# First batch's attention: exponentials turned by TensorE in float32 in place of float16 halves turned by DMA

## The chip, the cores and the metric

The kernel runs on one core of one Trainium2 chip. Five engines work beside each other, each through its own queue in order: TensorE (PE, its weight loads shown apart as PEld), VectorE (DVE), ScalarE (ACT), GpSimd (POOL) and SyncE (SP), which issues the DMAs here. They wait for each other by semaphores. The metric is the device time of one execution in microseconds (us); less is better.

## The reference

Clustered attention over 2 batches x 8 heads x 768 positions x 64 dimensions, then two feed-forward layers over the 1536 tokens.

```python
q_assign = np.argmax(np.einsum('bhsd,hcd->bhsc', q_n, c_n), axis=-1)   # q_n, k_n, c_n: normalised
k_assign = np.argmax(np.einsum('bhsd,hcd->bhsc', k_n, c_n), axis=-1)
mask = q_assign[:, :, :, None] == k_assign[:, :, None, :]
scores = np.where(mask, scale * np.matmul(q, k.transpose(0, 1, 3, 2)), -1000000000.0)
attn = np.exp(scores - np.max(scores, axis=-1, keepdims=True))
attn = attn / (np.sum(attn, axis=-1, keepdims=True) + 1e-09)
x = np.matmul(attn, v)                    # then tokens x 512
h = x @ w_in                              # 512 -> 2048
x = (h * np.clip(h + 3.0, 0.0, 6.0) / 6.0) @ w_out
for e in range(4):                        # 4 experts, 512 -> 1024 -> 512
    out += p[:, e:e + 1] * (np.maximum(x @ w1[e], 0.0) @ w2[e])
```

`w_in` and `w_out` arrive as 64-bit floats and are turned into 32-bit ones on the chip.

## The kernel before

The program is written as a list of tasks, each for one engine with an assumed duration, a due time (`prio`) and the buffers that it reads and writes. `Order.plan` places them one by one, by these assumed durations, and `emit` writes the instructions in that order. So the order of each queue is fixed beforehand, and a change of one task or of one assumed duration moves others. The table `PAR` holds due times, pool sizes and choices of engine.

The stages are: attention of the first batch (`a0`), the first layer of the first batch (`Moe1`, with the conversion of `w_in` and `w_out`, `conv_w`), its second layer (`Moe2`) with the attention of the second batch (`a1`) in its gaps, and the two layers of the second batch. Attention goes by pairs of heads (4) and blocks of 256 queries (3 a pair): 12 blocks, each of 4 units (2 heads x 128 queries), 48 units in all.

One unit of the first batch runs so:

- `scores` (L708): PE writes 128 x 768 scores into a tile `pss` (two PSUM banks, ring `ps_sa` of three) by four matmuls (L718, L720). Ahead of them stands a matmul of zeros, 384 columns wide, that is overwritten (`fill`, L716). DVE takes the row maximum (L725), ACT the exponential with the row sum (L726) into the float32 tile `e`.
- `sums` (L731): two one-column DVE instructions give the reciprocal of the row sum (L734, L735).
- `halves` (L737): the normalised `e` is written as two float16 tiles, the rounded value and the rest. By its letter in `ka` a unit does so as "P" (POOL L740, ACT L741, POOL L742), as "A" (ACT L745, DVE L749) or as "D" (POOL L747, DVE L749).
- a DMA transpose (L681, on SP's queue) turns the halves into `pt`.

When a block's four units are turned, `av` (L694) multiplies with `v`: 18 steps of two matmuls (one for each head, side by side in 64 columns of the array), since high and low halves of `pt` and of `v` make three products over six blocks of keys. L702 (ACT) and L704 (DVE) write the block's result `x1` as a rounded and a rest part. `values` (L628) loads `v` and makes its halves `vh` and `vl` (L636 to L655). `prep` (L516) makes ready what the scores of a pair read.

`conv_w` (L786) converts a tile of `w_in` or `w_out`: DMA load (L791), ACT L794, DVE L795, L796, L798, L800. Four of the 32 tiles fall in the attention stage, the other 28 behind it.

Of the kernel before, what the change touches and what calls it, by code (L numbers as in the profile page):

```python
# [25 lines left out]
def _f32(u):  # L26
# [23 lines left out]
    lead1=2.4290359447307104,  # L50
    vlead=-11.709535254235975,
    avp=-9.142989452549473,
    parts=3,
    ka=["APDPPDPDADPA", "PADPPAPAAPAP", "PPDPPDDAAPAA", "PDPDPDPDPPAD"],
    kb="DDDP",
    a_pool=dict(raw=2, nat=3, vr=1, sc=1, so=1, cs=2, oh=3, sm=2, e=6, p=3, pt=4, vh=2, vl=2, tiny=11, tv=4, stk=4),
    b_pool=dict(raw=2, nat=1, vr=1, sc=2, so=1, cs=1, oh=1, sm=2, e=2, p=2, pt=3, vh=1, vl=1, tiny=11, tv=4, stk=2),
    xba=[2, 2, 2, 1, 2, 1, 1, 2, 1, 2, 2, 1],
    xbb=1,
    loa="VP",  # L60
    lob="VV",
# [4 lines left out]
    nat0=-49.95,  # L66
    dup=["PPPP", "P"],
    dpx=2,
    fill=384,
    wo1=0,  # L70
    two=[0, 0],
    seq=[0, 1, 3, 2, 4, 5, 6, 7, 9, 10, 8, 11],
    btail=10.347963191960837,
    bu0=39.36802588487378,
# [258 lines left out]
def body(ctx: ExitStack, tc: tile.TileContext, qk, nat, vd, cent, w_in, w_out, probs, w1, w2, out):  # L333
# [23 lines left out]
    def pe(n, prio, fn, r, w, cols=0):  # L357
        return add("PE", n, prio, fn, r, w, cols=cols or 2400 * n)
# [4 lines left out]
    def dve(n, prio, fn, r, w, fast=False, ap=False):  # L363
        return add("DVE", 1e-3 * (n / (1.92 if fast else 0.96) + 68 + 60 * ap), prio, fn, r, w)

    def pool(n, prio, fn, r, w, ns=2.1):
        return add("POOL", 1e-3 * (n * ns + 150), prio, fn, r, w)

    def dma(nbytes, prio, fn, r, w):
        return add("SP", 0.52, prio, fn, r, w, dma=nbytes / 360e3)  # L370

    mm = lambda n: 1e-3 * (n / 2.4 + 2.5)


    g_c = o.group("left", keep=True)
# [22 lines left out]
    p_x2 = {n: Pool(f"x2{n}", 1, g_w) for n in "hl"}  # L398
    p_oa = Pool("oa", 1, g_w)
    p_g = Pool("g", 5, g_w1)  # L400
    p_s = [Pool("ps_sa", 3, g_pa, True), Pool("ps_sb", 2, g_ps, True)]
    p_v = [Pool("ps_va", 1, g_pa, True), Pool("ps_vb", 1, g_ps, True)]
    p_pm = [Pool("ps_ma", 1, g_pa, True), Pool("ps_mb", 3, g_pm, True)]
    p_m = p_pm[1]
# [71 lines left out]
    x1 = {}  # L476

    class Attn:
        def __init__(self, b, g, gp, n):
            self.b = b  # L480
            self.xb = max(PAR["xba"]) if b == 0 else PAR["xbb"]
            prep = ("raw", "nat", "vr", "sc", "so", "cs", "oh", "sm")
            P = lambda name: Pool(name + str(b), n[name], gp if name in prep else g)
            self.p = {k: P(k) for k in ("raw", "nat", "vr", "sc", "so", "cs", "oh", "sm", "e", "p", "pt", "vh", "vl", "tiny", "tv")}
            if b == 0:
                self.p["ohq"] = Pool("ohq", 1, gp)
            for k in ("qa", "qb", "ka", "kb"):
# [140 lines left out]
        def values(self, hp, p):  # L628
            b, st = self.b, self.pair[hp]
            vr = self.buf("vr", [128, 2, NT, D], F32)  # L630
            dma(393e3, p(0), lambda: nc.sync.dma_start(out=vr.t, in_=vd[b, hp]), [], [vr])
            tb = self.buf("tv", [128, 8], F32)
            am, inv, mx, dg = tb, tb, tb, tb
            vh, vl = self.buf("vh", [128, 2, NT, D], F16), self.buf("vl", [128, 2, NT, D], F16)
            for q in range(2):
                act(HS, p(1), lambda q=q: nc.scalar.activation(out=vh[:, q], in_=vr[:, q], func=AF.Abs, accum_out=am[:, q:q + 1]),  # L636
                    [vr], [(vh, q), (tb, 0)], acc=True)
            ps = Buf(p_pm[b], [2, 128], F32, "psam")
            pe(0.1, p(1), lambda: nc.tensor.transpose(ps.t, am[:, 0:2], ident.t), [(tb, 0)], [ps])
# [12 lines left out]
            for q in range(2):
                act(HS, p(2), lambda q=q: nc.scalar.activation(out=vh[:, q], in_=vr[:, q], func=AF.Copy, scale=inv[:, 6 + q:7 + q]),
                    [vr, (tb, 3)], [(vh, q)], ap=True)
                dve(HS, p(2), lambda q=q: nc.vector.scalar_tensor_tensor(  # L655
                    out=vl[:, q], in0=vr[:, q], scalar=inv[:, 6 + q:7 + q], in1=vh[:, q], op0=ALU.mult, op1=ALU.subtract),
                    [vr, (tb, 3), (vh, q)], [(vl, q)], ap=True)
            st["v"] = (vh, vl)

        def block(self, hp, blk, p, kinds, xb, avp):  # L660

# [69 lines left out]
        def sums(self, tb, n, p):  # L731
            keys = [(tb, 2 + i) for i in range(n)]
            rs = lambda: tb[:, 2:2 + n]
            dve(n, p, lambda: nc.vector.tensor_scalar(out=rs(), in0=rs(), scalar1=1e-9, scalar2=1.0 / PSC, op0=ALU.add, op1=ALU.mult), [], keys)  # L734
# [296 lines left out]
    for hp in range(NP):  # L1031
        t0 = when[hp, 0]
        lead = lambda x, t0=t0, hp=hp: t0 - (G["lead0"] + G["lead2"] * hp - G["lead1"] * x) if hp else -49.9 + 0.1 * x
        a0.prep(hp, lead, G["loa"] if hp else "VV")
        a0.values(hp, (lambda x, t0=t0: t0 - G["vlead"] - G["vlead2"] * hp + x) if hp else (lambda x: 3.0 + x))
        for blk in range(NBQ):
            a0.block(hp, blk, lambda i, t0=when[hp, blk]: t0 + i * T_UNIT, G["ka"][hp][4 * blk:4 * blk + 4], G["xba"][3 * hp + blk], G["avp"])

    t = T_A + NP * per * T_UNIT + 4.0
    stages = []  # L1040
# [125 lines left out]
```

## Time and profile before

| | |
|---|---|
| device time, median of 3 runs | 1071.14 us (1069.41 to 1074.32) |
| span of the profiled execution, first to last instruction | 1070.8 us |
| PE busy | 981.9 us (92%) |
| DVE busy | 781.6 us (73%) |
| ACT busy | 517.5 us (48%) |
| POOL busy | 496.9 us (46%) |
| mean granted TensorE clock | 0.962 of full speed |

The profile gives no time of the profiled execution but its span, which stands 0.3 us under the median of the runs. Busy shares are means over stages that differ, so stages are read apart. A granted clock of 1.0 is 2.4 GHz, 0.5 is 1.2 GHz; a value between is a mean over a stretch that had both. Busy times of PE are those of overlapping matmuls, so PE's rate is read from the starts of matmuls that follow each other.

### The profile page before, as it was taken

To read this page: it belongs to the slowest core of one execution; us is meant where nothing else is said; L and a number is where in the kernel's file an instruction comes from. 1 tells how busy PE (TensorE), PEld (TensorE's weight loads), DVE (VectorE), ACT (ScalarE), POOL (GpSimd) and SP (SyncE) were. 2 spreads that over 40 slices of the span, in tenths; PEclk is the share of its full clock that TensorE was granted. 3 is DMA by queue.
4 is the path that set the end of the run, shared out by engine and by line. 5 is a ranking of instruction groups with operands and counts; after the bars stand their busy time and mean duration, and the time that the engine had idled before them with its cause. 6 is when DMAs were issued, how large, how long until landed. Compare 5 with 4: busy or idle time off the path is not lost.

```text
span 1070.8 us, 15706 instructions
## 1 busy us (share of the span) xinstructions
PE 981.9 (92%) x5579; PEld 881.4 (82%) x5579; DVE 781.6 (73%) x1407; ACT 517.5 (48%) x969; POOL 496.9 (46%) x385
## 2 busy tenths in 40 slices
PE   3666787889899999999999999999999999999998
PEld 1555666788799888888898898999999999899987
DVE  8999995999635687478467356679888577766773
ACT  6676765545336446345255343565554334443330
POOL 3576963555346787255263444533442313333221
PEclk9777789899999999999999999999999999999999
DMA  8499799866205476257357347512221112212211
GB/s 262 108 194 193 152 180 219 265 206 221 69 1 169 148 164 150 90 142 142 99 132 129 97 97 167 138 42 77 62 86 50 62 58 79 80 48 71 76 44 59
DMA packets 192366, 129.34 MB, mean 121 GB/s; under 512 B 155488, under 2 KB 155488, under 8 KB 192288
## 3 DMA queue, kind: packets, MB, share of 16 engines
q1 hardware_dynamic: 192288, 128.34, 46.5%
q8 instruction: 44, 0.72, 0.3%
q14 instruction: 34, 0.28, 0.1%
HBM read 74.51 MB, written 11.53 MB: 80 GB/s over the span
## 4 chain that ended last, share of the span: by engine, by line
PE 51%; DVE 24%; DMA 10%; issue 6%; POOL 5%; ACT 3%; SPq 0%; POOLq 0%; DVEq 0%; ACTq 0%
PE psm L814 8%; PE psm L816 8%; PE psm L815 8%; DMA pt<-p 7%; DVE p L749 4%; PE psw L886 4%; PE psw L884 4%; PE psw L885 4%; PE psg L815 4%; PE psg L816 3%; PE psg L814 3%; DVE ut L725 3%; DVE wconv L795 2%; DVE wconv L798 2%; DVE wconv L800 2%
## 5 line engine op out<-in xcount | busy, mean ns | idle before, releaser
L758 POOL TENSOR_TENSOR w<-wraw,w 128x512 fp32r<-128x512 f32 x160 | 215.3, 1372 | 276.8 <-ACT w L757 269.9
L814 PE MATMUL psm<-w,h 128*128 128x512 f32 x384 | 152.0, 396 | 0.8 <-DVE h L997 0.8
L816 PE MATMUL psm<-w,h 128*128 128x512 f32 x384 | 150.8, 393 | 0.0
L815 PE MATMUL psm<-w,h 128*128 128x512 f32 x384 | 150.5, 392 | 0.0
L726 ACT ACTIVATE e<-pss,ut 128x768 f32<-128x768 f32 x96 | 86.0, 897 | 72.4 <-DVE ut L725 50.7
L757 ACT ACTIVATE w<-wraw 128x512 fp32r<-128x512 f32 x160 | 95.1, 627 | 25.7 <-DMA wraw<-in_w 12.2
L1012 DVE SCALAR_TENSOR_TENSOR oa<-psm,pr,oa 128x512 f32<-128x512 f32 x84 | 61.7, 746 | 56.2 <-PE psm L816 56.1
L749 DVE SCALAR_TENSOR_TENSOR p<-e,ut,p 128x768 f16<-128x768 f32 x62 | 87.5, 1417 | 19.0 <-POOL p L747 16.0
L814 PE MATMUL psm<-x2h,w 128*128 128x384 f32 x288 | 98.3, 341 | 0.6 <-DVE h L997 0.6
L816 PE MATMUL psm<-x2h,w 128*128 128x384 f32 x288 | 96.8, 336 | 0.0
L815 PE MATMUL psm<-x2l,w 128*128 128x384 f32 x288 | 96.5, 335 | 0.0
L815 PE MATMUL psg<-g,w 128*128 128x384 f32 x256 | 88.5, 346 | 6.0 <-DVE g L951 4.4
L725 DVE TENSOR_REDUCE ut<-pss 128x1 f32<-128x768 f32 x96 | 90.1, 945 | 4.6 <-PE pss L720 4.5
L814 PE MATMUL psg<-g,w 128*128 128x384 f32 x256 | 87.8, 343 | 3.2 <-DVE t L946 2.3
L816 PE MATMUL psg<-g,w 128*128 128x384 f32 x256 | 87.2, 341 | 1.7 <-POOL w L758 1.7
L814 PEld LDWEIGHTS psm<-w,h 128*128 128x128 f32 x384 | 72.1, 188 | 16.8 <-issue 1.8
L816 PEld LDWEIGHTS psm<-w,h 128*128 128x128 f32 x384 | 72.1, 188 | 16.0 <-DVE h L997 0.2
L815 PEld LDWEIGHTS psm<-w,h 128*128 128x128 f32 x384 | 72.2, 188 | 12.8
L997 DVE SCALAR_TENSOR_TENSOR h<-psm,h 128x384 fp32r<-128x384 f32 x72 | 39.6, 553 | 46.6 <-ACT h L996 46.5
L996 ACT ACTIVATE h<-psm 128x384 fp32r<-128x384 f32 x72 | 34.8, 487 | 79.3 <-PE psm L816 76.6
L747 POOL TENSOR_SCALAR p<-e,ut 128x768 f16<-128x768 f32 x49 | 47.0, 961 | 54.8 <-DMA pt<-p 24.4
L718 PEld LDWEIGHTS pss<-ka,qa 128*128 128x128 f32 x192 | 40.6, 220 | 30.8 <-issue 27.6
(185 smaller groups left out, 2508.2 us busy)
## 6 DMA issues: line engine op xcount, KB each, us to landing
wraw<-in_w SPq DMA_DIRECT2D x128, 256.0 KB, 3.2
r<-in_w_in SPq DMA_DIRECT2D x16, 512.0 KB, 4.9
r<-in_w_out SPq DMA_DIRECT2D x16, 512.0 KB, 4.4
nat<-in_nat SPq DMA_DIRECT2D x16, 384.0 KB, 4.1
raw<-in_qk SPq DMA_DIRECT2D x16, 384.0 KB, 4.0
scr_i<-wconv SPq DMA_DIRECT2D x16, 256.0 KB, 2.3
scr_o<-wconv SPq DMA_DIRECT2D x16, 256.0 KB, 3.0
wraw<-scr_i SPq DMA_DIRECT2D x16, 256.0 KB, 2.8
```

Of the source, the lines that this page charges most:

```text
L725: dve(S, p, lambda: nc.vector.tensor_reduce(out=nb(), in_=ps[:, :, 0:HS], axis=AX.XY, op=ALU.max, negate=True), [ps], [(tb, n)])
L726: act(S, p, lambda: nc.scalar.activation(out=e.t.rearrange("p (a b) -> p a b", a=2), in_=ps[:, :, 0:HS], func=AF.Exp, bias=nb(), scale=1.0 ...
L747: pool(S, p, lambda: nc.gpsimd.tensor_scalar(out=pp[:, j, 0], in0=e.t, scalar1=rs(), scalar2=1.0, op0=ALU.mult, op1=ALU.mult), [e, key], [ ...
L749: dve(S, p, lambda: nc.vector.scalar_tensor_tensor(out=pp[:, j, 1], in0=e.t, scalar=rs(), in1=pp[:, j, 0], op0=ALU.mult, op1=ALU.subtract) ...
L757: act(512, p, lambda: nc.scalar.activation(out=w[:, 0], in_=raw.t, func=AF.Copy), [raw], [(w, 0)])
L758: pool(512, p, lambda: nc.gpsimd.tensor_tensor(out=w[:, 1], in0=raw.t, in1=w[:, 0].bitcast(F32), op=ALU.subtract), [raw, (w, 0)], [(w, 1)])
L814: nc.tensor.matmul(o_, ah, bh, start=i == 0, stop=False)
L815: nc.tensor.matmul(o_, ah, bl, start=False, stop=False)
L816: nc.tensor.matmul(o_, al, bh, start=False, stop=i == 3)
L884: nc.tensor.matmul(o_, ah, bh, start=k == 0, stop=False)
L885: nc.tensor.matmul(o_, ah, bl, start=False, stop=False)
L1012: dve(512, p, lambda: nc.vector.scalar_tensor_tensor(out=oa[:, t], in0=ps.t, scalar=q, in1=oa[:, t], op0=ALU.mult, op1=ALU.add), [ps, pr], ...
```

## The change

For the first batch `block` gives way to `turned`. POOL normalises `e` in place in float32 for all 48 units. PE turns it by six float32 transposes a unit (L693 of the changed kernel) into two PSUM tiles `pst` of 384 columns (a ring of two); ACT (L700) and, for every fifth, DVE (L702) copies them to a float32 `pt`. `av` (L709) is then six steps of two float32 matmuls with `v` as it was loaded. The halves of `e` and of `v`, the scaling of `v` and the DMA transposes are gone for this batch. The matmul of zeros is gone (`fill=0`). The ring of scores goes from three tiles to two, which makes room for `pst`. The planner's assumed duration of every matmul rises by 10.5 ns (`mm`), so orders shift elsewhere too. The second batch's attention keeps its halves.

```diff
+    avpa=-8.0,
-    ka=["APDPPDPDADPA", "PADPPAPAAPAP", "PPDPPDDAAPAA", "PDPDPDPDPPAD"],
+    kn="PPPPPP",
+    kt="AAAAD",
-    a_pool=dict(raw=2, nat=3, vr=1, sc=1, so=1, cs=2, oh=3, sm=2, e=6, p=3, pt=4, vh=2, vl=2, tiny=11, tv=4, stk=4),
+    a_pool=dict(raw=2, nat=3, vr=3, sc=1, so=1, cs=2, oh=3, sm=2, e=7, pt=5, tiny=11, stk=4),
-    xba=[2, 2, 2, 1, 2, 1, 1, 2, 1, 2, 2, 1],
-    fill=384,
+    fill=0,
+    trp=3.0,
+    trh=2,
+    parta=6,
...
-    mm = lambda n: 1e-3 * (n / 2.4 + 2.5)
+    mm = lambda n: 1e-3 * (n / 2.4 + 13.0)
...
-    p_s = [Pool("ps_sa", 3, g_pa, True), Pool("ps_sb", 2, g_ps, True)]
+    p_s = [Pool("ps_sa", 2, g_pa, True), Pool("ps_sb", 2, g_ps, True)]
+    p_tr = Pool("ps_ta", PAR["trh"], g_pa, True)
...
             dma(393e3, p(0), lambda: nc.sync.dma_start(out=vr.t, in_=vd[b, hp]), [], [vr])
+            if b == 0:
+                st["v"] = vr
+                return
...
+        def turned(self, hp, blk, p, avp):
+            b, st = self.b, self.pair[hp]
+            pts, vr = [], st["v"]
+            for q in range(2):
+                qa, qb, ka, kb = st["heads"][q]
+                ptile = self.buf("pt", [128, JQ, NT, 128], F32)
+                pts.append(ptile)
+                for j in range(JQ):
+                    i = q * JQ + j
+                    tb = self.buf("tiny", [128, 8], F32, "ut")
+                    e = self.scores(qa, qb, ka, kb, blk * BQ + j * 128, tb, 0, p(i))
+                    self.sums(tb, 1, p(i), 1.0)
+                    sc = lambda eng, e=e, tb=tb: eng.tensor_scalar(out=e.t, in0=e.t, scalar1=tb[:, 2:3], scalar2=1.0, op0=ALU.mult, op1=ALU.mult)
+                    if PAR["kn"][i % len(PAR["kn"])] == "P":
+                        pool(S, p(i), lambda sc=sc: sc(nc.gpsimd), [(tb, 2)], [e], ns=0.956)
...
+                    nh = PAR["trh"]
+                    for h in range(nh):
+                        ps = Buf(p_tr, [128, 2 // nh, 512], F32, "pst")
+                        def turn(e=e, ps=ps, h=h):
+                            for t in range(NT // nh):
+                                x = (h * (NT // nh) + t) * 128
+                                nc.tensor.transpose(ps[:, t // 3, t % 3 * 128:t % 3 * 128 + 128], e[:, x:x + 128], ident.t)
+                        pe(NT // nh * 0.109, p(i) + PAR["trp"], turn, [e], [ps], NT // nh * 128)
...
+                        if PAR["kt"][((blk * 4 + i) * nh + h) % len(PAR["kt"])] == "A":
+                            act(S // nh, p(i) + PAR["trp"], lambda src=src, dst=dst: nc.scalar.activation(out=dst(), in_=src(), func=AF.Copy), [ps], [key], ps=True)
+                        else:
+                            dve(S // nh, p(i) + PAR["trp"], lambda src=src, dst=dst: nc.vector.tensor_copy(out=dst(), in_=src()), [ps], [key])
+            ps = Buf(p_v[b], [128, BQ], F32, "psv")
+            parts = PAR["parta"]
+            def av(part):
+                for t in range(part * NT // parts, (part + 1) * NT // parts):
+                    for q in range(2):
+                        nc.tensor.matmul(ps[64 * q:64 * q + 64], vr[:, q, t], pts[q][:, :, t], start=t == 0, stop=t == NT - 1)
...
-            a0.block(hp, blk, lambda i, t0=when[hp, blk]: t0 + i * T_UNIT, G["ka"][hp][4 * blk:4 * blk + 4], G["xba"][3 * hp + blk], G["avp"])
+            a0.turned(hp, blk, lambda i, t0=when[hp, blk]: t0 + i * T_UNIT, G["avpa"])
```

Three places show how the queues change. First PE in the later part of the stage. Before, each unit is a weight load and matmul of zeros (`junk`) and the four score matmuls, and between units stands a block's run of 36 float16 matmuls, of which the first pair of rows is shown:

```order
L716 LDWEIGHTS ident_b
L716 MATMUL pss<-junk,ident_b 128x384
L718 MATMUL pss<-ka,qa 128x384 x2
L720 MATMUL pss<-kb,qb 128x384 x2
L694 LDWEIGHTS vh
L694 MATMUL psv<-pt,vh 64x256
```

Now six transposes of an older unit stand between the scores of two units, and a block's product with `v` is one row of twelve matmuls:

```order
L693 MATMUL pst<-ident,e 128x128 x6
L778 MATMUL pss<-ka,qa 128x384 x2
L780 MATMUL pss<-kb,qb 128x384 x2
L709 MATMUL psv<-pt,vr 64x256 x12
L693 MATMUL pst<-ident,e 128x128 x6
```

PE has no row of zeros left, and gets one row of transposes for each unit. Second, SP at the end of the stage, where the loads of the first `w_out` tiles (`r`) stand. Before:

```order
L681 DMA_TRANSPOSE pt<-p 128x12x128
L681 DMA_TRANSPOSE pt<-p 128x24x128 x6
L681 DMA_TRANSPOSE pt<-p 128x12x128 x8
L791 DMA r_2032<-in_w_out 128x1024
L791 DMA r_2034<-in_w_out 128x1024
```

Now they follow the last small copies (`so` to `qb`, `kb`) of the fourth pair's preparation:

```order
L630 DMA qb<-so 16x768
L630 DMA kb<-so 16x768
L851 DMA r_1927<-in_w_out 128x1024
L851 DMA r_1929<-in_w_out 128x1024
```

The loads had the last 15 DMA transposes ahead of them, and have none now. Third, DVE from the stage's last row maximum (`ut<-pss`) to the first row of the 28 conversions (`wconv`). Before:

```order
L725 TENSOR_REDUCE ut<-pss 128x1
L749 SCALAR_TENSOR_TENSOR p<-e,ut,p 128x768
L735 RECIPROCAL ut<-ut 128x1
L734 TENSOR_SCALAR ut<-ut 128x1
L735 RECIPROCAL ut<-ut 128x1
L704 SCALAR_TENSOR_TENSOR x1l_710<-psv,sv,x1h_698 128x256
L734 TENSOR_SCALAR ut<-ut 128x1
L735 RECIPROCAL ut<-ut 128x1
L749 SCALAR_TENSOR_TENSOR p<-e,ut,p 128x768
L946 SCALAR_TENSOR_TENSOR t<-t,psg_1846 128x384
L749 SCALAR_TENSOR_TENSOR p<-e,ut,p 128x768
```

Two further `x1l` and `t` rows follow there before `wconv`. Now, with `t<-t,psg` the first layer's rows as before:

```order
L785 TENSOR_REDUCE ut<-pss 128x1
L794 TENSOR_SCALAR ut<-ut 128x1
L795 RECIPROCAL ut<-ut 128x1
L794 TENSOR_SCALAR ut<-ut 128x1
L795 RECIPROCAL ut<-ut 128x1
L717 TENSOR_TENSOR x1l_616<-psv,x1h_606 128x256
L702 COPY pt<-pst 128x384
L1006 SCALAR_TENSOR_TENSOR t<-t,psg_1748 128x384
L1006 SCALAR_TENSOR_TENSOR t<-t,psg_1853 128x384
L855 TENSOR_SCALAR wconv<-wconv 128x512
L856 TENSOR_SCALAR wconv<-wconv 128x512
L717 TENSOR_TENSOR x1l_616<-psv,x1h_606 128x256
```

The three rows L749 are gone from between, and the conversions now stand ahead of the last block's `x1l`.

## Rows read from the trace of the kernel before

**Rows 1.** Stretches: length, busy PE PEld DVE ACT POOL, granted clock, DMA share, GB/s.

```profile
26.40:161.40 135.00, 97.77 (x617) 76.84 (x618) 129.62 (x246) 94.32 (x174) 94.58 (x68) 0.76 0.82 165
161.40:183.90 22.50, 17.01 (x152) 14.16 (x151) 9.75 (x20) 11.63 (x21) 8.95 (x8) 0.92 0.93 191
183.90:282.00 98.10, 84.92 (x437) 78.38 (x436) 96.42 (x145) 48.83 (x91) 48.27 (x33) 0.95 0.67 219
290.00:1071.00 781.00, 765.92 (x4288) 700.08 (x4286) 521.11 (x937) 343.38 (x655) 333.50 (x264) 1.00 0.36 95
```

**Rows 2.** Timeline of DVE, first conversion instruction behind the attention stage.

```profile
183.38 0.43 DVE L795 TENSOR_SCALAR wconv<-wconv 128x512 f32<-128x512 f32 x1 [1.71 <-ACT wconv L794]
```

**Rows 3.** Timeline of PE, the first and the last unit's scores: start, length.

```profile
26.38 1.09 PE L718 MATMUL pss<-ka,qa 128*128 128x384 f32 x2
...
160.86 0.65 PE L718 MATMUL pss<-ka,qa 128*128 128x384 f32 x2
```

**Rows 4.** Groups by line, 26.4 to 161.4 us: busy, mean ns, idle before.

```profile
L742 POOL TENSOR_TENSOR p<-e,p 128x768 f16<-128x768 f32 x20 | 35.9, 1800 | 5.7 <-ACT p L741 5.4
L749 DVE SCALAR_TENSOR_TENSOR p<-e,ut,p 128x768 f16<-128x768 f32 x22 | 35.6, 1631 | 0.4 <-POOL p L747 0.4
L740 POOL TENSOR_SCALAR e<-e,ut 128x768 f32<-128x768 f32 x20 | 22.7, 1136 | 19.6 <-DVE ut L735 6.9 <-ACT e L726 5.9 <-DVE ut L734 3.8
L716 PE MATMUL pss<-junk,ident_b 128*128 128x384 bf16 x48 | 19.6, 408 | 26.7 <-ACT e L726 26.6
L741 ACT ACTIVATE p<-e 128x768 f16<-128x768 f32 x20 | 16.7, 840 | 9.0 <-POOL e L740 6.7 <-DMA pt<-p 2.2
L747 POOL TENSOR_SCALAR p<-e,ut 128x768 f16<-128x768 f32 x12 | 12.6, 1047 | 3.3 <-DMA pt<-p 2.0 <-issue 1.1 <-POOL e L740 0.2
L745 ACT ACTIVATE p<-e,ut 128x768 f16<-128x768 f32 x11 | 10.3, 932 | 3.5 <-DMA pt<-p 2.0 <-DVE ut L735 1.1 <-ACT e L726 0.2
L655 DVE SCALAR_TENSOR_TENSOR vl<-vr,tv,vh 128x384 f16<-128x384 f32 x8 | 8.3, 1072 | 0.8 <-ACT vh L653 0.8
L653 ACT ACTIVATE vh<-vr,tv 128x384 f16<-128x384 f32 x8 | 4.5, 605 | 4.0 <-DVE tv L651 4.0
L565 ACT ACTIVATE sc<-psc 128x384 f32<-128x384 f32 x3 | 1.5, 488 | 2.3 <-PE psc L562 2.3
```

**Rows 5.** The chain that ended last, 140 to 190 us.

```profile
167.82 5.45 DMA pt<-p
...
178.56 6.01 DMA r<-in_w_out
```

**Rows 6.** Timeline of SP's queue at the end of the attention stage.

```profile
151.49 25.94 SPq L681 DMA_TRANSPOSE pt<-p  x10
177.48 2.48 SPq L791 DMA_DIRECT2D r<-in_w_out  x4
```

**Rows 7.** The tile `pss`: who works on it, durations ns min/median/max.

```profile
L725 DVE TENSOR_REDUCE ut<-pss x96: 930/946/959, 28.9 to 668.6; 128x1 f32<-128x768 f32 x96
L726 ACT ACTIVATE e<-pss,ut x96: 877/901/910, 30.5 to 669.7; 128x768 f32<-128x768 f32 x96
L726 ACT ACTIVATION_READ_ACCUMULATOR e<-pss,ut x96: 184/192/211, 31.3 to 670.5; 128x1 f32 x96
```

**Rows 8.** Timeline of PE at clock 1.0, later: scores, float32 matmuls, transposes.

```profile
603.89 0.85 PE L562 MATMUL psc<-raw,ct 128*32 128x384 f32 x8
...
612.36 0.49 PE L570 MATMUL psct<-ident,sc 128*128 128x128 f32 x3
...
625.81 0.52 PE L718 MATMUL pss<-ka,qa 128*128 128x384 f32 x2
...
626.51 0.40 PE L814 MATMUL psm<-w,h 128*128 128x512 f32 x1
```

**Rows 9.** One tile's instructions: durations ns min/median/max (`psct`, then `psc`).

```profile
L570 PE MATMUL psct<-ident,sc x24: 270/272/476, 11.5 to 612.6; 128*128 128x128 f32 x24
...
L562 PE MATMUL psc<-raw,ct x64: 486/510/849, 7.4 to 604.3; 128*32 128x384 f32 x64
```

More of the change, by code (lines that the diff above doesn't have):

```diff
@@ L480, in __init__ @@
             self.b = b
-            self.xb = max(PAR["xba"]) if b == 0 else PAR["xbb"]
-            prep = ("raw", "nat", "vr", "sc", "so", "cs", "oh", "sm")
+            self.xb = PAR["xbb"]
+            prep = ("raw", "nat", "sc", "so", "cs", "oh", "sm") + (("vr",) if b else ())
             P = lambda name: Pool(name + str(b), n[name], gp if name in prep else g)
-            self.p = {k: P(k) for k in ("raw", "nat", "vr", "sc", "so", "cs", "oh", "sm", "e", "p", "pt", "vh", "vl", "tiny", "tv")}
+            self.p = {k: P(k) for k in n if k != "stk"}
             if b == 0:
@@ L658, in values @@
             st["v"] = (vh, vl)
+        def turned(self, hp, blk, p, avp):
[14 more added lines that the diff above has]
+                    else:
+                        dve(S, p(i), lambda sc=sc: sc(nc.vector), [(tb, 2)], [e], fast=True)
+                    nh = PAR["trh"]
[6 more added lines that the diff above has]
+                        pe(NT // nh * 0.109, p(i) + PAR["trp"], turn, [e], [ps], NT // nh * 128)
+                        src = lambda ps=ps: ps[:, :, 0:HS]
+                        dst = lambda ptile=ptile, j=j, h=h: ptile[:, j].rearrange("p (a t) k -> p a (t k)", a=2)[:, h * 2 // nh:(h + 1) * 2 // nh] if nh == 1 else ptile[:, j].rearrange("p (a t) k -> p a (t k)", a=2)[:, h:h + 1]
+                        key = (ptile, (j, h))
+                        if PAR["kt"][((blk * 4 + i) * nh + h) % len(PAR["kt"])] == "A":
+                            act(S // nh, p(i) + PAR["trp"], lambda src=src, dst=dst: nc.scalar.activation(out=dst(), in_=src(), func=AF.Copy), [ps], [key], ps=True)
+                        else:
+                            dve(S // nh, p(i) + PAR["trp"], lambda src=src, dst=dst: nc.vector.tensor_copy(out=dst(), in_=src()), [ps], [key])
[5 more added lines that the diff above has]
+                        nc.tensor.matmul(ps[64 * q:64 * q + 64], vr[:, q, t], pts[q][:, :, t], start=t == 0, stop=t == NT - 1)
+            for part in range(parts):
+                pe(NT / parts * (BQ * 4 / 2400 + 0.02), p(4 + part * 4 / parts) + avp, lambda part=part: av(part), pts + [vr], [ps], NT / parts * BQ * 4)
+            sl = slice(blk * BQ, blk * BQ + BQ)
+            xh, xl = x1[b]
+            key = (hp, blk)
+            act(BQ, p(6), lambda: nc.scalar.activation(out=xh[:, hp, sl], in_=ps.t, func=AF.Copy), [ps], [(xh, key)], ps=True)
+            dve(BQ, p(6), lambda: nc.vector.tensor_tensor(
+                out=xl[:, hp, sl], in0=ps.t, in1=xh[:, hp, sl].bitcast(F32), op=ALU.subtract), [ps, (xh, key)], [(xl, key)])
@@ L729, in scores, with sums @@
             return e
[L731 removed]
+        def sums(self, tb, n, p, unit=1.0 / PSC):
             keys = [(tb, 2 + i) for i in range(n)]
             rs = lambda: tb[:, 2:2 + n]
[L734 removed]
+            dve(n, p, lambda: nc.vector.tensor_scalar(out=rs(), in0=rs(), scalar1=1e-9, scalar2=unit, op0=ALU.add, op1=ALU.mult), [], keys)
             dve(n, p, lambda: nc.vector.reciprocal(out=rs(), in_=rs()), [], keys)
```

## The prediction

> **What bounds the kernel now.** I read the stretches first, since a share over the whole span mixes stages. They show four: attention of the first batch to its last scores, its end, the conversion stage, and the rest [rows 1]. From 290 us on PE is busy 765.9 of 781 us at clock 1.00: PE sets the pace there, and the change touches little in it. From 183.9 to 282 us DVE is busy 96.4 of 98.1 us with 28 tiles of `conv_w`: DVE sets the pace, and the change takes none of this away. So the change can win only by letting DVE begin these tiles earlier than now, at 183.38 us [rows 2].
>
> What holds that start? The first scores run at 26.38 us and the last at 160.86 us [rows 3]: 48 units in 134.5 us, 2.80 us each. There DVE is busy 129.6 of 135.0 us (96%), PE 97.8 at a mean clock of 0.76, and the DMA engines have a share of 0.82 [rows 1]: DVE is the bound, DMA is close. PE's largest wait is ahead of the matmul of zeros, 26.6 of 26.7 us for ACT's exponential [rows 4], which itself waits for DVE's maximum. From the last scores to 183.38 us another 22.5 us pass in which DVE is busy only 9.75 us [rows 1]. The chain shows why: it goes through a turn of `pt` of 5.45 us and then the load of `w_out`, 6.01 us from 178.56 us [rows 5]. SP's queue shows that this load was issued at 177.48 us, right behind ten DMA transposes that held the queue for 25.94 us [rows 6].
>
> **The change part by part.** I cost the stretch to the last scores engine by engine, then the end.
>
> *DVE.* Gone are L749 (35.6 us) and L655 (8.3 us) [rows 4]. New are 16 copies of 384 columns from PSUM, for which the nearest row is ACT's copy of the same size, 0.488 us [rows 4]: 7.8 us. So 129.6 - 43.9 + 7.8 = 93.5 us. L749 took 1.63 us in the mean and L655 1.07, though L749's 768 columns are as many as L725's at 0.946 [rows 7]; if it was POOL's subtraction L742 that held DVE back, other DVE rows get shorter too. I count nothing for that.
>
> *ACT.* Gone: L741, L745 and L653, 31.5 us. New: 80 copies, 39.0 us [rows 4]. So 94.3 + 7.5 = 102 us at most, since some copies come behind the last scores.
>
> *POOL.* Gone: L742, L747 and 20 L740, 71.2 us; new: 48 normalisations at 1.136 us, 54.5 us [rows 4]. So 78 us.
>
> *PE at full clock.* Scores: 0.70 us for four matmuls, from the starts at 625.81 and 626.51 us [rows 8]; 48 make 33.6. The matmul of zeros (19.6 us of overlapping busy time) is gone. Transposes: three in 0.49 us [rows 8], one alone 0.272 [rows 9], so one every 0.109 us; 261 of the 288 stand ahead of the last scores: 28.4. Float32 products: eight instructions of 384 columns, four side by side in each of two passes, took 0.85 us, one alone about 0.49 [rows 8, 9], so a pass is about 0.36 - 0.02 = 0.34 us. A step of `av`, 256 columns in two passes with both heads side by side, is 2 x 0.34 x 256/384 = 0.45 us; six make 2.7 a block, and ten blocks ahead of the last scores 27. If the heads did not lie side by side, a block would cost twice that; the row of eight speaks against it. Other work (cluster scores, turns of one-hot rows, first `psg`): about 5. Sum: 94 us. At half clock all of this takes 188.
>
> No engine is left with more than 102 us where DVE had 129.6, and the DMA transposes are gone. Two things keep the sum from being the time. The clock: 0.76 in this stretch, 0.95 in the next, where PE is busy 87% [rows 1]. PE's work for a unit now nearly fills it, so I take 0.90, nearer the second: 94 / 0.90 = 104 us. And waiting for each other in fixed queues: the bound engine was busy 96% here before; now three engines of similar load must keep step over shorter rings, so I take 0.90: 104 / 0.90 = 116 us, or 2.4 us a unit. The last scores come at 26.4 + 116 = 142 us.
>
> *The end.* SP's loads of `w_out` stand behind no transposes any more, so they don't hold DVE. By the order, PE has between the last scores and the second `psg` tile 27 transposes (2.9 us), one `av` (2.7) and seven groups of three 384-column matmuls (0.175 each as in the scores, 3.7); then ACT and DVE pass over it in some 1.5 us. With the scores' own 0.7 that is 11.5 us in place of 22.5. DVE begins to convert at 153.5 us, 30 us earlier than now.
>
> *Behind it.* The conversion stage is bound by the same 28 tiles and shifts as a whole. The new assumed matmul duration moves some instructions in later stages; PE's idle time there is 15.1 us in all [rows 1], so I put this at 0, with bounds of 5 to either side.
>
> **Sum:** 1070.8 - 30 = 1040.8 for the profiled execution; the median of the runs is 0.3 higher: **1041 us**.
>
> Bounds: if every unit still took 2.80 us, the end alone would give 183.4 - (160.9 + 11.5) = 11 us: 1060. If PE ran at full clock without a wait, the last scores would come at 120.4 and conversion would start 51 us earlier: 1020.
>
> **The rivals.**
>
> *The clock falls (slower).* Granted clock was 0.76 in this stretch with PE's zeros in it [rows 1]; those go, and a fifth to a third of PE's time becomes transposes. If transposes ran at 1.2 GHz throughout and the rest at 0.76: (65.6 / 0.76 + 56.8) / 0.90 = 159 us, last scores at 185, conversion at 200: 17 us later, 1088. It decides from a mean clock of about 0.72 on (94 / 0.72 / 0.90 = 145 us, which with the end makes 183.4). For it: the stage had low clocks before. Against it: a stretch in which PE is dense had 0.95, and the transposes in the trace run at 0.109 us each at clock 1.0 [rows 8]. The Trainium skill, "TensorE: Matmul & The Clock Gate", Part 4: PE-mode transpose, says that transposes do not count as work in the way that brings full clock. By that rule this rival would hold; the trace has no stretch with many transposes, so no row settles it.
>
> *The ring of two scores (no change).* A `pss` tile is held from the scores (0.70 us) over the maximum (0.946) and the exponential with its sum (1.09) [rows 7, 8]: 2.74 us, for two units at a time 1.4 us a unit. But each works behind others in its queue: six transposes on PE (0.65), two copies on ACT (0.98), a copy on DVE (0.49), which makes 4.9 us, or 2.4 a unit, the pace I forecast. If an `av` (2.7 us) stood in every second turn of the ring as well, it would be 6.2, 3.1 a unit: last scores at 175, conversion at 187, 3 us later; with the odd turn faster, no change, about 1071. Against it: during `av` ACT and DVE can finish the tiles in hand.
>
> *A larger gain.* All of PE's stretch at full clock with hardly a wait: 1020, as above.
>
> **How the numbers follow.** Forecast (1025 to 1060) 0.70, larger gain 0.10, ring with no change (1066 to 1076) 0.10, clock and slower 0.10. The range 1020 to 1066 leaves out the last two and little else. Faster by over 0.5% (below 1066; about what a measurement of this kernel can tell from no change) 0.80, within 0.5% 0.10, slower 0.10.
>
> **What would show it.** In the profile of the changed kernel: last scores at 142 us and first conversion at about 153 us, then a conversion stage of some 98 us as before; DVE busy some 80% to the last scores, not 96%; granted clock near 0.9 there; transposes at 0.109 us, a block's product in 2.7 us; no wait of the first L855 for the `w_out` load. The prediction is wrong if PE's clock stays at 0.7, if PE waits for ACT's exponential in most units (the ring), if a float32 product takes 5 us a block, or if the conversion stage gets longer because its weights' loads wait for memory that attention still holds.

## The result, and the profile after

The changed kernel takes 1085.17 us (median of 4 runs, 1081.77 to 1088.90) against 1072.73 (1069.41 to 1074.57) for the kernel before: ratio 1.0125, 95% interval 1.009 to 1.0159. It is slower; 1041 was forecast. The profiled execution spans 1081.5 us.

Stretches of the changed kernel first, columns as in [rows 1]: the first two rows have cuts of [rows 1], the others are cut at the changed kernel's own marks (first scores, those of the thirteenth unit, last scores, first conversion, first product of the second layer `psm`, first product of the second batch `psg`, end).

```profile
26.40:161.40 135.00, 119.05 (x805) 92.37 (x805) 96.56 (x214) 99.88 (x214) 66.51 (x64) 0.97 0.23 69
290.00:1071.00 781.00, 756.71 (x4215) 689.64 (x4214) 521.11 (x929) 339.67 (x648) 325.66 (x258) 1.00 0.36 93
...
25.30:65.70 40.40, 31.62 (x167) 24.59 (x163) 30.84 (x70) 25.90 (x54) 19.06 (x18) 0.92 0.34 97
65.70:151.20 85.50, 78.59 (x576) 60.86 (x574) 62.73 (x136) 67.49 (x145) 44.62 (x43) 1.00 0.22 66
151.20:165.90 14.70, 14.44 (x108) 11.14 (x107) 3.90 (x13) 9.29 (x21) 4.74 (x5) 1.00 0.01 2
165.90:322.90 157.00, 137.44 (x730) 131.97 (x729) 115.05 (x179) 71.01 (x134) 78.21 (x54) 0.95 0.40 132
322.90:680.60 357.70, 341.99 (x2013) 302.70 (x2012) 222.28 (x394) 158.85 (x305) 185.84 (x152) 0.99 0.56 130
680.60:1081.50 400.90, 388.43 (x2041) 359.31 (x2039) 287.64 (x515) 164.93 (x313) 123.45 (x93) 1.00 0.20 66
```

The last three of these stretches in the kernel before:

```profile
183.40:331.00 147.60, 134.43 (x720) 127.44 (x719) 115.29 (x178) 70.22 (x132) 72.02 (x53) 0.97 0.47 154
331.00:677.80 346.80, 338.41 (x2014) 300.24 (x2013) 221.29 (x394) 159.28 (x305) 187.64 (x152) 1.00 0.56 134
677.80:1070.80 393.00, 386.52 (x2041) 359.28 (x2039) 283.12 (x515) 164.80 (x313) 123.05 (x93) 1.00 0.21 68
```

Attention does end earlier: conversion begins at 165.9 us in place of 183.4. Then 9.4, 10.9 and 7.9 us are lost in three stretches that the change was not meant for: -17.5 + 28.2 = +10.7 us, the difference of the spans. In the last two, PE has nearly the same instructions. It is busy a little longer (342.0 against 338.4 us, 388.4 against 386.5) and stands idle more: 357.7 - 342.0 = 15.7 us against 346.8 - 338.4 = 8.4, and 12.5 against 6.5.

Marks in the changed kernel's timeline, which answer to [rows 2] and [rows 3]: on PE the last unit's scores, the last two block products with `v` and products of 384 columns behind them, on DVE the first conversion:

```profile
151.22 0.59 PE L778 MATMUL pss<-ka,qa 128*128 128x384 f32 x2
...
153.80 2.81 PE L709 MATMUL psv<-pt,vr 128*64 128x256 f32 x24
...
162.29 2.81 PE L709 MATMUL psv<-pt,vr 128*64 128x256 f32 x24
...
165.66 0.33 PE L874 MATMUL psg<-x1h,w 128*128 128x384 f32 x1
165.83 0.33 PE L875 MATMUL psg<-x1l,w 128*128 128x384 f32 x1
166.01 0.33 PE L876 MATMUL psg<-x1h,w 128*128 128x384 f32 x1
...
166.35 0.33 PE L875 MATMUL psg<-x1l,w 128*128 128x384 f32 x1
...
165.87 0.43 DVE L855 TENSOR_SCALAR wconv<-wconv 128x512 f32<-128x512 f32 x1 [2.30 <-ACT wconv L854]
```

And the new operations, from the views of the tiles `pst` and `psv` (durations min/median/max in ns):

```profile
L693 PE MATMUL pst<-ident,e x288: 270/273/476, 34.9 to 161.0; 128*128 128x128 f32 x144
L700 ACT ACTIVATE pt<-pst x80: 472/491/518, 37.4 to 161.3; 128x384 f32<-128x384 f32 x80
L702 DVE COPY pt<-pst x16: 548/548/558, 42.4 to 158.3; 128x384 f32<-128x384 f32 x16
...
L709 PE MATMUL psv<-pt,vr x288: 379/379/431, 45.1 to 164.7; 128*64 128x256 f32 x144
```

The costs of these operations were forecast well: a transpose 273 ns alone (272 in [rows 9]), ACT's copy 491 (488), and a block's product 2.8 us in the timeline (2.7).

Last, what PE waited for in the second layer of the first batch with the second batch's attention (us in total, times, longest), in the changed kernel; the last two rows are of the stretch behind it, 680.6 to 863.5 us:

```profile
PE psv L754 <- DMA pt<-p: 13.0, 8, 3.4
PE psm L876 <- DVE h L1057: 2.3, 1, 2.3
...
PE psg L875 <- DVE g L1011: 4.9, 4, 2.0
PE psg L874 <- DVE acc L1024: 1.8, 2, 1.1
```

The same in the kernel before, 331 to 677.8 us:

```profile
PE psv L694 <- DMA pt<-p: 6.5, 7, 1.9
PE psm L814 <- DVE h L997: 0.8, 1, 0.8
```

PE waits twice as long for the second batch's `pt` (13.0 and 6.5 us), although the change leaves this attention's instructions as they were.

### The profile page after: what moved, and what is told of

It reads as the page before. It is cut to its first block, busy times and chain, and to the rows that moved or that the text cites. A ratio compares the mean times of both kernels' runs of the same rounds, so it can differ in the third digit from the quotient of the medians.

```text
span 1081.5 us, 15814 instructions
## 1 busy us (share of the span) xinstructions
PE 1000.8 (93%) x5663; PEld 894.4 (83%) x5663; DVE 744.3 (69%) x1361; ACT 513.5 (47%) x990; POOL 465.4 (43%) x376
## 4 chain that ended last, share of the span: by engine, by line
PE 60%; DVE 18%; DMA 8%; ACT 6%; issue 5%; POOL 3%; SPq 0%; DVEq 0%; POOLq 0%; ACTq 0%
PE psm L874 9%; PE psm L876 9%; PE psm L875 9%; DMA pt<-p 5%; PE psg L875 4%; PE psg L876 4%; PE psg L874 4%; PE psw L946 4%; PE psw L944 4%; PE psw L945 4%; PE psv L709 3%; PE pst L693 2%; DVE p L809 2%; ACT e L786 2%; PE pss L778 2%
## 5 line engine op out<-in xcount | busy, mean ns | idle before, releaser
L874 PE MATMUL psm<-w,h 128*128 128x512 f32 x384 | 152.4, 397 | 0.0
L785 DVE TENSOR_REDUCE ut<-pss 128x1 f32<-128x768 f32 x96 | 90.5, 950 | 17.5 <-PE pss L780 16.6
L681 POOL TENSOR_SCALAR e<-e,ut 128x768 f32<-128x768 f32 x48 | 44.7, 933 | 53.3 <-DVE ut L795 31.9
L874 PE MATMUL psg<-x1h,w 128*128 128x384 f32 x160 | 56.9, 356 | 10.8 <-DVE t L1006 10.6
L778 PE MATMUL pss<-ka,qa 128*128 128x384 f32 x192 | 56.3, 376 | 8.0 <-ACT e L786 8.0
```

Of the source, the lines that this page charges most:

```text
L681: sc = lambda eng, e=e, tb=tb: eng.tensor_scalar(out=e.t, in0=e.t, scalar1=tb[:, 2:3], scalar2=1.0, op0=ALU.mult, op1=ALU.mult)
L778: nc.tensor.matmul(ps[:, f, 0:HS], qa[:, qs], ka[:, f * HS:f * HS + HS], start=True, stop=False)
L785: dve(S, p, lambda: nc.vector.tensor_reduce(out=nb(), in_=ps[:, :, 0:HS], axis=AX.XY, op=ALU.max, negate=True), [ps], [(tb, n)])
L874: nc.tensor.matmul(o_, ah, bh, start=i == 0, stop=False)
```

## The experiments

The two kernels and all eighteen experiments, with the stretches of each one's profile. "assumed" is the constant in the planner's matmul duration (n/2.4 + constant, ns); "scores 13" means that the first batch's scores keep 13. Columns a to d: start of the conversion; from there to the first `psm`; from there to the second batch's first `psg`; from there to the end.

| kernel | median us (range) | ratio to before, 95% | a | b | c | d |
|---|---|---|---|---|---|---|
| before (2.5) | 1072.73 (1069.41 to 1074.57) | | 183.4 | 147.6 | 346.8 | 393.0 |
| after (13) | 1085.17 (1081.77 to 1088.90) | 1.0125, 1.009 to 1.0159 | 165.9 | 157.0 | 357.7 | 400.9 |
| e1: after, 2.5 | 1066.38 (1062.98 to 1068.52) | 0.9944, 0.9918 to 0.997 | 162.2 | 157.0 | 352.4 | 393.2 |
| e2: before, 13 | 1099.45 (1098.37 to 1100.49) | 1.0255, 1.0233 to 1.0278 | 178.4 | 158.0 | 357.5 | 402.4 |
| e3: after, scores 13, rest 2.5 | 1064.75 (1063.53 to 1066.77) | 0.9934, 0.991 to 0.9957 | 167.7 | 152.8 | 351.0 | 393.5 |
| e7: e3, second batch's layers 13 | 1070.24 (1068.23 to 1073.24) | 0.9987, 0.9969 to 1.0004 | 168.2 | 152.8 | 351.6 | 398.9 |
| e5: scores 13, rest 8 | 1078.18 (1074.55 to 1080.77) | 1.0054, 1.0035 to 1.0073 | 166.0 | 154.4 | 362.1 | 395.2 |
| e6: scores 13, rest -8 | 1048.56 (1046.94 to 1050.60) | 0.9779, 0.9745 to 0.9812 | 165.4 | 149.4 | 339.9 | 392.2 |
| e9: before, -8 | 1062.86 (1061.93 to 1065.74) | 0.9923, 0.99 to 0.9947 | 184.6 | 144.2 | 339.9 | 391.7 |
| e12: after (13), other engines +8% | 1066.54 (1065.94 to 1068.29) | 0.9953, 0.9936 to 0.9969 | 166.0 | 155.8 | 350.7 | 392.1 |
| e4: after, tiles late | 1083.29 (1078.89 to 1084.80) | 1.0098, 1.0065 to 1.0132 | 161.2 | 160.8 | 358.3 | 402.6 |
| e8: e3, tiles late | 1058.76 (1057.61 to 1059.49) | 0.9872, 0.984 to 0.9904 | 160.5 | 152.8 | 351.1 | 393.3 |
| e10: e6, tiles late | 1043.77 (1041.69 to 1049.14) | 0.9745, 0.9715 to 0.9776 | 160.1 | 149.6 | 340.2 | 391.7 |
| e11: e10 with -20 | 1043.63 (1042.38 to 1045.32) | 0.9737, 0.9718 to 0.9756 | 162.7 | 147.4 | 336.8 | 396.1 |
| e13: e10, ring 12 | 1047.87 (1047.51 to 1049.57) | 0.9781, 0.9759 to 0.9804 | 163.4 | 151.8 | 340.4 | 392.2 |
| e14: e3, ring 12 | 1063.55 (1062.56 to 1066.63) | 0.9934, 0.991 to 0.9958 | 165.2 | 152.4 | 350.8 | 392.7 |
| e15: before, ring 12 | 1071.84 (1070.69 to 1073.57) | 1.0005, 0.9993 to 1.0017 | 183.2 | 148.0 | 345.5 | 393.0 |
| e16: e10, t early | 1041.97 (1038.71 to 1045.30) | 0.9729, 0.9699 to 0.976 | 161.2 | 145.8 | 339.6 | 391.7 |
| e17: e3, t early | 1060.52 (1059.59 to 1061.11) | 0.9901, 0.9885 to 0.9918 | 167.0 | 148.8 | 350.6 | 392.7 |
| e18: after, t early | 1080.30 (1076.62 to 1082.13) | 1.0093, 1.0072 to 1.0113 | 165.0 | 153.3 | 355.9 | 400.6 |

Each ratio is to runs of the kernel before on the same chip, whose median lay between 1071.2 and 1072.7 us.

### The assumed matmul duration (e1, e2, e3, e7)

The theory: the loss comes from `mm`, which reorders the later stages, and not from the new attention.

```diff
-    mm = lambda n: 1e-3 * (n / 2.4 + 13.0)     # e1; e2 is the reverse, in the kernel before
+    mm = lambda n: 1e-3 * (n / 2.4 + 2.5)
```
```diff
+    mm = lambda n, c=2.5: 1e-3 * (n / 2.4 + c)     # e3
-            pe(4 * mm(HS) + ..., p, score, ...)
+            pe(4 * mm(HS, 13.0 if self.b == 0 else 2.5) + ..., p, score, ...)
+        MMC[0] = 13.0 if st.b == 1 else 2.5            # e7, on top of e3: set where the layers are listed
```

> The changed kernel with the planner's assumed matmul duration as before (n/2.4 + 2.5 ns); nothing else is undone. Theory M (the assumed duration reorders the later stages and costs there what the first attention won): from the second batch's first scores to the end 702 us as in the kernel before, not 722; 1060 to 1068 us in all. Rival H (the new attention itself, by its earlier end or by what it leaves behind, slows the later stages): 722 us again there, about 1085 us in all.

> The kernel before with the assumed matmul duration of the change (n/2.4 + 13 ns) and nothing else of it. Theory M: slower by 13 to 20 us, 1085 to 1092 us, lost after 360 us. Rival H: within 4 us of the kernel before, 1068 to 1076 us.

> The changed kernel with the new assumed duration only for the first batch's score matmuls, and the old one for every other matmul. Theory M: the first attention as in the changed kernel (last scores at about 151 us) and the later stages as in the kernel before: 1060 to 1068 us. Rival H: about 1085 us. If it differs from e1_mm_old by more than 5 us, the order within the first attention matters too.

> As e3_mm_split, but the new 13 ns also for the matmuls of the second batch's two layers, so that the order differs from e3_mm_split from there on alone. Theory M: these layers take the 7 us longer that they take in the changed kernel from 690 to 820 us, with PE waiting there for DVE's rest parts: 1070 to 1074 us. Rival: they are long there only because of what the stages before leave behind: 1063 to 1067 us.

With the old constant and nothing else undone the changed kernel is faster than before, and the new constant alone makes the kernel before slower by 2.55%, more than was expected (1099.45 us against 1085 to 1092). Column d is the cleanest: 400.9 to 402.4 us with 13 (after, e2) and 393.0 to 393.5 with 2.5 (before, e1, e3), whichever attention stands ahead; e7, where 13 holds for the second batch's layers alone, has b and c of e3 and 398.9 in d.

The traces also hold the order of each queue. From 10 us behind the first `psm` to the end, all five engines have their instructions, by tile, in the same order in e2 as in the changed kernel, and in e3 in the same order as in the kernel before. So the order of these stages is set by the constant alone, and the new attention ahead of them changes nothing of it.

### Luck of an order, or a ratio (e5, e6, e9, e12)

The theory: a planner that believes PE to be faster than it is places the work that feeds PE earlier, which keeps a margin. Rival: each constant gives another order, good or bad by chance. e5 and e6 set 8.0 and -8.0 as e3 sets 2.5; e9 sets -8.0 for every matmul of the kernel before, as e2 sets 13. e12 keeps 13 and raises the assumed durations of the other three engines behind the attention.

```diff
-        return add("DVE", 1e-3 * (n / (1.92 if fast else 0.96) + 68 + 60 * ap), prio, fn, r, w)
+        return add("DVE", 1e-3 * FS[0] * (n / (1.92 if fast else 0.96) + 68 + 60 * ap), prio, fn, r, w)
...                                                    (ACT and POOL likewise)
+    FS[0] = 1.08                                      # ahead of the layers' tasks; 1.0 till then
```

> As e3_mm_split, but the assumed overhead of a matmul outside the first attention is 8.0 ns, between the old 2.5 and the new 13. Theory A (a PE that the planner believes faster than it is makes it place the feeding instructions of DVE and ACT earlier than PE needs them; the closer to the truth, the less margin): between the two, 1069 to 1080 us. Rival L (any new order is as good as another, the old one was lucky): no relation to the number, as likely above 1085 or below 1066 as between.

> As e3_mm_split, but with an assumed overhead of -8 ns, so that the planner believes PE still faster than with 2.5. Theory A: not slower than e3_mm_split (1065 us), 1055 to 1066 us. Rival L: above 1070 us as likely as not.

> The kernel before, with only the planner's assumed duration of every matmul lowered from n/2.4 + 2.5 to n/2.4 - 8.0 ns. Theory A (a planner that believes TensorE faster than it is places the work that feeds TensorE earlier, and so keeps a margin): faster than before by about what the changed kernel gained from 2.5 to -8, 16 us: 1055 us (1048 to 1062), PE's waits for pt in the second layer of the first batch down from 6.5 us to 1 to 4 us. Rival L (the times at 13, 8, 2.5 and -8 were luck of the changed kernel's order): within 5 us of 1071, or above. With either, the worth of the new attention at -8 is the distance of this run to the changed kernel's 1049 at -8; at 2.5 it was 6 us.

> The changed kernel with its 13 ns kept, and in its place the assumed durations of VectorE, ScalarE and GpSimd raised by 8% for all work behind the first batch's attention. Theory A (it is the ratio of assumed durations, TensorE against the engines that feed it, that sets the margin): 13 ns on 160 is about 6.5% against 2.5 ns, so most of the loss comes back: 1063 to 1073 us. Rival L, or a cause in the absolute assumed time of TensorE (against DMA and semaphores, which stay as they are): no gain, 1080 to 1092 us.

13, 8, 2.5 and -8 give 1085, 1078, 1065 and 1049 us (the last three with the scores at 13), and in the kernel before 13, 2.5 and -8 give 1099, 1073 and 1063: a trend of the whole time, not scatter. Its size was not foreseen: e6 gained more than expected (1048.56 against 1055 to 1066), e9 less (1062.86, just outside 1048 to 1062). Nor does every stretch follow it: at 8, c is 362.1 us, longer than the 357.7 at 13. e12 decides between the ratio of assumed durations and PE's assumed time by itself: with the 13 kept, raising the other side gives all of it back (1066.54 against e1's 1066.38, d 392.1). So the ratio counts. PE's waits for `pt` in the stretch c are shorter, too. Rows of e12, e6 and e9 in this order, which answer to the `pt` rows above (13.0 in after, 6.5 in before):

```profile
PE psv L756 <- DMA pt<-p: 9.0, 7, 2.7
...
PE psv L754 <- DMA pt<-p: 2.7, 2, 1.4
...
PE psv L694 <- DMA pt<-p: 1.9, 4, 1.4
```

That what feeds PE stands earlier can be counted in PE's own order. Between the last scores of a block of the second batch and the first of its products with `pt` stand, in the mean of the 12 blocks, 51.8 products of the layers at 13 (the changed kernel and e2), 53.5 at 8, 58.0 at 2.5 (before and e3), 60.5 at -8 (e6 and e9), 66.5 at -20 (e11) and 56.8 in e12. The exponentials, the halves and the DMA transpose of the block have that much work of PE to hide behind.

### The first twelve units, and how far the margin goes (e4, e8, e10, e11)

The first 12 units take 40.4 us, 3.4 each; from the scores of the thirteenth to those of the last it is 85.5 us, 2.44 each. In the first of these stretches the four tiles of `w_in` take 12.1 us of DVE (L855 to L860). The experiment plans their loads behind the first pair's third block, so behind these 12 units (the texts below name the block differently):

```diff
-                out=r.t, in_=src[:, k]..., [], [r])
+                out=r.t, in_=src[:, k]..., [(x1[0][1], (0, 2))] if which == 0 else [], [r])
```

> The changed kernel with the first four conversion tiles planned behind the first batch's fourth block (by a dependence that the planner sees). Theory C (their 12 us on DVE slow the first 12 units): the 12 units take 30 us in place of 37.7, last scores at 143 to 146 us, 1077 to 1081 us in all if the later order stays. Rival (the preparation of the second pair and the ring of two scores set the first units' pace): 12 units in 36 us or more, last scores at 150 us or later, 1085 us or more.

> e3_mm_split and e4_conv_late together. If what the late conversion wins in the first attention (last scores 4 to 6 us earlier) is carried to the end: 1059 to 1062 us. If the conversion stage takes it back, as it took 5 us of the first attention's 15 in e3_mm_split: 1063 to 1066 us.

> The changed kernel with -8.0 ns outside the first batch's scores, and the first four conversion tiles planned behind the first batch's last block, both at once. Theory A with theory C's later tiles adding up: the tiles gave 6 us at 2.5 (1065 to 1059), so 1042 us (1038 to 1046). Rival: both draw on the same room on VectorE in the conversion stage, and the tiles give nothing here: 1047 to 1052.

> As the run at -8.0 with late tiles, with -20.0 ns in place of -8.0. Theory A: the margin only helps while TensorE still waits; at -8 it waited 3.1 us in the second layer of the first batch and 1.9 us in the first layer of the second, so at most 5 us are left there: 1036 to 1044 us, hardly faster than the run at -8. Rival L (order luck): no trend, 1050 to 1075. A turn (the planner starts work too early and rings fill) would show as over 1046 us.

In e4 the first 12 units take 30.2 us (24.8 to 55.0) in place of 40.4, 2.5 each, as theory C has it; from there to the last scores at 146.6 it is 91.5 us in place of 85.5, since the tiles now lie there, and the conversion stage begins 4.7 us earlier. On the changed kernel itself that can't be told from no change (1083.29, between the two forecasts; the ranges overlap). On e3 it comes through: 1058.76 against 1064.75. On e6 the medians are 1043.77 against 1048.56, but one of four runs of e10 lies within e6's range. At -20 nothing more is won: c falls by 3.4 us and d rises by 4.4 against e10, so the trend ends about there.

### Why the conversion stage is longer (e13 to e18)

At the smaller constants column b is still longer behind the new attention: 149.4 against 144.2 at -8, 152.8 (e3) against 147.6 at 2.5. At 13 it is not: 157.0 against 158.0 (e2). DVE has a hole there: from 225.9 to 245.9 us of the changed kernel it is busy 12.2 of 20 us, while ACT waits 8.0 us for one product. First theory (T): the ring of converted tiles is full.

```diff
-    wrc = [Pool("wrca", 4, g_l0), Pool("wrcb", 9, g_m[0])]
+    wrc = [Pool("wrca", 4, g_l0), Pool("wrcb", 12, g_m[0])]
```

> The run at -8 with late tiles, with the ring of conversion tiles (wconv) behind the attention stage raised from 9 to 12. Theory T (the conversion stage did not shift as a whole because the tiles' ring is full while TensorE works through a run of products, so that VectorE has no tile to convert for some 5 to 8 us): VectorE's busy share in the conversion stage rises from 95.5 of 102.3 us to over 96 of about 98, and the time falls by 3 to 5 us: 1039 us (1037 to 1041). Rival U (the tiles wait for the split weights' rings, which stay at 4, or for ScalarE's wait for the products itself): the hole stays and the time is 1042 to 1046.

> The changed kernel with 13 ns for the first batch's scores alone and 2.5 elsewhere (1064.75 us), with the ring of conversion tiles raised from 9 to 12. Theory T: 3 to 5 us less, 1060 to 1062, with a conversion stage of about 98 us in place of 102.3. Rival U: 1063 to 1067, stage of 101 us or more.

> The kernel before with the ring of conversion tiles raised from 9 to 12, as the control: its VectorE had no hole in the conversion stage (96.4 of 98.1 us busy). Theory T: no room to gain, within 2 us of 1071. Rival (a larger ring changes the planner's order everywhere and moves the time by that): outside 1069 to 1074, by which the two runs above would have to be read with that much doubt.

T falls, and with it a step of the prediction. The larger ring does shorten the conversion: in e14 it takes 94.0 us from its first instruction on DVE to its last in place of 102.3, and the last starts at 259.2 us, not 270.0. But the second layer starts only 2.9 us earlier (317.6 against 320.5, where the conversion itself began 2.5 us earlier), and b stays at 152.4. The conversion is even shorter than T's 98 us, but the time is that of rival U (1063.55). e13 misses both forecasts: its 1047.87 is 4.1 us above e10, though the ranges touch. e15, the control, came out as expected. So the end of the conversion does not set the start of the second layer.

What is left is PE, busy 134 to 137 us of b in the kernel before and the changed one. In e3 PE has this wait at the start of the stretch (timeline):

```profile
168.92 0.34 PE L876 MATMUL psg<-x1h,w 128*128 128x384 f32 x1
177.27 0.69 PE L874 MATMUL psg<-x1h,w 128*128 128x384 f32 x1 [8.01 <-DVE t L1006]
177.76 0.53 PE L875 MATMUL psg<-x1l,w 128*128 128x384 f32 x1
178.08 0.53 PE L876 MATMUL psg<-x1h,w 128*128 128x384 f32 x1
...
167.74 0.43 DVE L855 TENSOR_SCALAR wconv<-wconv 128x512 f32<-128x512 f32 x1 [2.30 <-ACT wconv L854]
...
176.34 0.41 DVE L856 TENSOR_SCALAR wconv<-wconv 128x512 int32<-128x512 int32 x1
176.68 0.54 DVE L1006 SCALAR_TENSOR_TENSOR t<-t,psg 128x384 f32<-128x384 f32 x1
...
167.70:177.70 10.00, 1.99 (x10) 1.67 (x10) 9.92 (x17) 4.94 (x11) 3.51 (x3) 0.80 0.54 170
```

PE's next product needs a bank that `t` reads, and `t` stands in DVE's queue behind conversions. In the kernel before these first products lay in the 22.5 us in which DVE was busy only 9.75 us [rows 1]; PE's longest wait for `t` was 3.3 us there and 2.4 behind it. But the new attention is not needed for a long one. In e2, the kernel before with 13, PE waits for `t` in the stretch b (us in total, times, longest):

```profile
PE psg L814 <- DVE t L946: 14.6, 5, 9.8
```

Theory V: this wait sets the stretch.

```diff
-            act(MB, p, ... [ps], [t], ...)                    # t, first chunk of the first batch's first layer
-            dve(MB, p, ... [ps], [t])
+            act(MB, p - 40.0 if b == 0 and c == 0 else p, ... [ps], [t], ...)
+            dve(MB, p - 40.0 if b == 0 and c == 0 else p, ... [ps], [t])
```

> The run at -8 with late tiles (1043.77 us), with the due times of t's two instructions (ScalarE L1005, VectorE L1006) 40 us earlier for the first chunk of the first batch's first layer, so that VectorE does the third of them behind four conversion instructions and not behind twelve. Theory V (the stretch from the first conversion to the second layer is set by TensorE, which stands idle at its start for 8.0 us because that t is queued behind conversions, and then runs 20 products or so at half clock): the long wait falls from 8.0 to 2 or 3 us and the time falls by 4 to 7 us: 1039 us (1036 to 1041). Rival U (VectorE's conversions set that stretch after all, or another wait takes the place): 1042 to 1047.

> The same edit on the changed kernel with 13 ns for the first batch's scores alone and 2.5 elsewhere (1064.75 us, with the same wait of 8.0 us). Theory V: 1058 to 1061, the stretch from the first conversion to the second layer 146 to 149 us in place of 152.8. Rival U: 1063 to 1068.

> The same edit on the changed kernel as it is (1085.17 us; its wait for that t is 5.9 us). Theory V: 3 to 5 us less, 1080 to 1082. Rival U: 1083 to 1088.

V holds for the stretch. The same place in e17, with the windows of its first 10 us:

```profile
170.66 0.44 PE L874 MATMUL psg<-x1h,w 128*128 128x384 f32 x1 [2.14 <-DVE t L1006]
...
167.00:177.00 10.00, 7.86 (x36) 7.54 (x35) 9.96 (x16) 5.22 (x10) 4.64 (x3) 0.83 0.46 142
```

The wait falls from 8.01 to 2.14 us, PE is busy 7.86 and not 1.99 of the first 10 us, and b falls by 4.0, 3.8 and 3.7 us at the three settings (e17, e16, e18). The medians are 4.2, 1.8 and 4.9 us lower. e17 and e18 lie in V's range; e16 does not (1036 to 1041 was expected), and its time can't be told from e10, whose range it overlaps. e16 has the lowest median of all, 1041.97 us.

## Why the prediction was wrong

By its own steps, in the profiled executions (the sum was 1040.8, the span is 1081.5):

| step | forecast | measured | off by |
|---|---|---|---|
| last scores | 142 | 151.2 | +9.2 |
| the end, to the first conversion | 11.5 | 14.7 | +3.2 |
| first conversion to the second layer ("shifts as a whole") | 147.6 | 157.0 | +9.4 |
| the rest (assumed duration "at 0, with bounds of 5") | 739.8 | 758.6 | +18.8 |

**The step that turned the sign is the last: the assumed duration.** The prediction took PE's 15.1 us of idle time for the room in which a new order could gain or lose. That bounds a gain; idle time has no upper bound, and in c alone it is now 15.7 us. By e1 and e3 the constant costs about 20 us of the median, by e2 27; in spans, e3 has 14 us less than after behind the first `psm`, and 4.2 less in b. The remaining 5 us behind the first `psm`, most of them in c, are there in e3 although its queues have the same order as the kernel before; at 13 and at -8 there is no such rest (c is 357.7 and 357.5, and 339.9 in e6 and e9). Its cause stays open.

**"Shifts as a whole" failed** because DVE being 98% busy was taken for the bound of what follows. The second layer starts when PE has gone through the first one, whose products wait for `t` in DVE's queue: e14 and e17 show it. The 9.4 us have two sources that don't simply add up. With the old constant 5.2 us are left (e3), of which an earlier `t` takes 4.0 (e17). With 13 an earlier `t` takes 3.7 (e18), and the kernel before loses 10.4 us there by the constant alone (e2). That the new attention costs PE the quiet stretch in which its first products met a DVE with little to do fits the traces at 2.5 and -8; it was not tested apart.

**The pace** came out right where no tiles are converted (2.44 us a unit, 2.4 forecast), but in part by luck. The clock was 1.00 there, not 0.90, and PE's sum gives 1.96 of the 2.44 us (94 us / 48), so that waits and work left out of the sum made up 20%, not 10%: two errors cancelled. The pace was wrong for the first 12 units (3.4), where DVE does conversions; e4 shows that these 12 take 2.5 each without the tiles, and that 6.0 of the 10.2 us return where the tiles go. **The end** has two block products behind the last scores (153.80 and 162.29 us), not one: 2.8 of the 3.2 us.

**Rivals.** The clock did not fall: 0.97 where 0.76 was before, and 1.00 from 65.7 to 165.9 us. From 65.7 to 151.2 us some 207 of PE's 576 recorded matmuls are transposes. The Trainium skill ("TensorE: Matmul & The Clock Gate", Part 4: PE-mode transpose) says that transposes don't count as work towards full clock. Mixed with the other products they did not lower it here; no longer stretch of this trace has transposes alone, so it does not settle the rule itself. The ring of two scores cost 4.4 us of waits in those 85.5 us, not the pace. The loss came through none of the rivals, but through waits in stages that the change was not meant for.

What held: the engines' loads from the first scores to the last, 25.3 to 151.2 us (DVE 93.6 us against 93.5 forecast, ACT 93.4 against at most 102, POOL 63.7 against 78, its normalisation faster than before, 905 ns from 65.7 us on against 1136), no wait of the first conversion for `w_out`, and that the new attention gains. At equal constants it is worth 14 us at 13 (e2 to after) and at -8 (e9 to e6, whose scores keep 13), and 5 to 6 at 2.5 (before to e1).

## What to carry to other kernels

A planner's assumed duration is a setting of the order, not a description: here a figure near the measured one (n/2.4 + 13) costs 19 to 27 us against one that is 10.5 ns too low, so a change that "only corrects" such a figure is tried by itself, apart from the change of the work. When a stage is pulled forward, ask which engine the next stage really waits for, and what quiet stretch it used: a busy engine at the seam need not be the one. Idle time of the bound engine limits what a new order can win, never what it can lose.

## What the runs showed of the hardware

In a run of products at clock 1.00, 384-column matmuls follow each other every 0.173 to 0.175 us (the rows at 165.66 to 166.35 above), which is 384/2.4 + 13 to 15 ns. Float32 transposes and float32 products in close succession left the granted clock at 1.00, 2.4 GHz, for 100 us (65.7 to 165.9). Behind an idle stretch of 8.0 us PE comes back at the lower level: in e3 the granted clock is 0.50, 1.2 GHz, from 177.7 to 180.0 us, and the products at 177.76 and 178.08 follow each other in 0.32 us. So the wait costs more than its own length.
